# The last spreading of the inverses issued behind their sending, and the last four tiles sent in the order 0, 2, 1, 3: a kernel of attention and a gated linear unit

## The chip, the cores and the metric

The kernel runs on one core of a Trainium2 chip. The metric is the device time of one launch in microseconds; smaller is better. The kernel before takes 1583.95 us, the median of 3 runs (1583.82 to 1584.93). The engines are named as in the profile: PE (TensorE, matmuls; PEld is its loading of weights), DVE (VectorE), ACT (ScalarE), POOL (GpSimd) and SP (SyncE, which here issues all DMAs; a row with SPq is SP's queue).

## The reference

Two branches share the input `x` (2048 rows of 512) and are mixed row by row by a sigmoid gate. The attention has 32 query heads of 16 columns and a single head of keys and values.

```python
g = sigmoid((x * gate_w).sum(-1, keepdims=True))
# a: q in 32 heads of 16; one k, one v
scores = einsum("bhqd,bkd->bhqk", q, k) * 16 ** -0.5
o = einsum("bhqk,bkd->bhqd", softmax(scores), v)
a = o.reshape(1, 2048, 512) @ wo
# b: GLU with a sigmoid gate, 1792 wide
b = (sigmoid(x @ w_gate) * (x @ w_up)) @ w_down
return g * a + (1 - g) * b
```

## The kernel before

**Tiles and units.** The 2048 rows are cut into four blocks of 512 (NB), and the attention of a block into 8 units of four heads (NG), 32 units in all (NU). Operands that need float32 accuracy are held as a high and a low part, and a product is made of three matmuls: high by high, high by low, low by high. The contraction of most matmuls is split over the top and the bottom 64 rows of the array, so two matmuls run beside each other, one in each half. A unit has three phases: score matmuls whose maxima DVE takes (L1141, L1143), score matmuls again whose exponentials ACT takes (L1150, L1152), and groups of 8 value matmuls (L1008, `values`) over 16 chunks of keys.

**What becomes of a unit's result.** The value matmuls give, for each of four heads, 16 columns and the sum of the exponentials. ACT and POOL gather them in `ou` (L1015, L1022). Then, for unit u:

- `store` (L1030, L1031) writes the sums and the results to DRAM (`sd`, `od`);
- `sums` (L1036) reads the sums back in a shape that uses all partitions, `invert` (L1045) takes their inverses on DVE;
- `send_inverse` (L1049) writes the inverses to DRAM (`rd`);
- `spread` (L1055) reads each inverse back, repeated over the 16 rows of its head, into `bc`. For unit NU-2 alone it does so for both halves of the partitions, and also reads the results `od` into `vd` (L1057), so it issues four DMAs there, each of 128 KB;
- `divide` multiplies the two on POOL (L1063) and splits the product into the high and the low part of `o` (L755, L756).

Units are divided in pairs. Of the last pair, unit NU-2 goes through `divide` alone; unit NU-1 stays in its PSUM bank and is handled by the tail. `o` of unit NU-2 is multiplied by the last rows of `wo` (held as `we` in two parts) in jobs of kind "e": L1115 in `fill`, 12 matmuls, added by DVE (L1072).

**What sets the order.** All instructions are emitted in an order worked out ahead. `State` is a planner: it goes through the written string ORDER, one code a step, and each code names what PE does next (a value group, or a matmul for each half of the array). The planner keeps a clock for each engine and for SP and the DMAs. Work that follows from something (a store, an inverse, a spread) is an event with a due time, and is emitted at the first step whose time is past it; POOL's work is a list of tasks, run when the planner's POOL is free. Each engine then runs its own instructions strictly in the order in which they were emitted; SP too, so a DMA issue that waits holds up every issue behind it.

**The half-turn markers.** A job accumulates into two banks, and the two halves of the array change banks in the middle. Where one half has ended its first bank, `fill` places an empty instruction on SP (`nc.sync.nop()`, L1119) that waits for PE's matmul, and the other half's first matmul into that bank waits for it.

**The events that the change touches.** `send` and `issue` advance the planner's SP and DMA clocks and return the time at which a transfer counts as landed (SP's end + SMALL at least); SAFE is 300 more. `send_inverse` makes `spread` due at that time; `spread` makes the task `divide` due 2 * SAFE after its own. Between the emission of `send_inverse` and that of `spread` for unit NU-2, one marker of L1119 is emitted.

**The tail.** After the last step, unit NU-1 is transposed, divided and transposed back (L1178 to L1191), multiplied by its 64 rows of `wo` (L1196), and added to the four last output tiles: tile 1 by ACT and POOL (L1202, L1203), tiles 0, 2 and 3, in this order, by DVE (L1205). SP then sends the four tiles (L1207), in the order 0, 1, 2, 3, each [128, 512] in float32 (256 KB).

Of the kernel before, what the change touches and what calls it, by code (L numbers as in the profile page):

```python
# [12 lines left out]
ALU = mybir.AluOpType  # L13
# [4 lines left out]
S, D, H, DH, F = 2048, 512, 32, 16, 1792  # L18
P = 128
# [7 lines left out]
NU = NB * NG  # L27
# [30 lines left out]
ISSUE, SMALL, TEN_KB, LAST, SAFE, SURE = 185, 750, 20, 300, 300, 150  # L58
# [64 lines left out]
class State:  # L123
# [170 lines left out]
    def event(self, what, args):  # L294
        self.acts.append((what, *args))
        if what == "load_x":
            self.x_loaded[args[0]] = self.send(KC, 1024)
        elif what == "store_q":
            at = self.send(2, 512)
            self.q_ready[tuple(args)] = at  # L300
            self.ba_release(("query", *args), at)
        elif what == "send_max":
            self.after(self.issue(SEND_SQUARE, 16) + SAFE, "place_max", *args)
        elif what == "max_square":
            self.after(self.on("dve", self.now, SQUARE) + TAIL, "send_max", *args)
        elif what == "place_max":
            self.max_ready[args[0]] = self.issue(PLACE, 16) + 150
        elif what == "store":
            at = self.sums_free[args[0] % OU] = self.issue(470, 264) + SAFE
            self.after(at, "sums", *args)  # L310
        elif what == "sums":
            self.after(self.issue(430, 136) + 2 * SAFE, "invert", *args)
        elif what == "invert":
            self.after(self.on("dve", self.now, INVERSE), "send_inverse", *args)
        elif what == "send_inverse":
            self.after(self.send(1, 8) + SAFE, "spread", *args)
        elif what == "spread":
            u = args[0]
            at = self.issue(250, 128)
            if u % 2 or u == NU - 2:  # L320
                self.task(2, at + 2 * SAFE, "divide", u)
        elif what == "out":
            self.tile_free[self.tile_of[tuple(args)]] = self.send(1, 256)
# [401 lines left out]
def tile_kernel(ctx, tc, x_in, wq, wkv, wo, wg, wu, wd, consts_in, out):  # L725
    nc = tc.nc
# [445 lines left out]
    n0 = (NB - 1) * NT  # L1172
    spare = lambda name: ap.tile([P, TB], F32, tag="p", name=name, bufs=PB)
    end, rest = banks[end], [bank for i, bank in enumerate(banks) if i != end]
    ps = rest[3:]
# [16 lines left out]
    for i in range(2):  # L1192
        for j in range(4):
            for t in (2 * i, 2 * i + 1):
                r, m = HALF[t % 2], slice(32 * j, 32 * j + 32)
                nc.tensor.matmul(ps[t][m, :], o[i][r, m], WS["last"][r], start=True, stop=True)  # L1196
    BL = [BA.pop((NB - 1, t)) for t in range(NT)]
    for t in (1, 0, 2, 3):
        ba, g = BL[t], gsig[:, n0 + t:n0 + t + 1]
        if t == 1:  # L1200
            pa = spare("pa_last")
            nc.scalar.activation(pa, ps[t], AF.Copy, scale=g)  # L1202
            nc.gpsimd.tensor_tensor(ba, ba, pa, op=ALU.add)  # L1203
        else:
            nc.vector.scalar_tensor_tensor(ba, ps[t], g, ba, op0=ALU.mult, op1=ALU.add)  # L1205
    for t in (0, 1, 2, 3):
        nc.sync.dma_start(out[(n0 + t) * P:(n0 + t + 1) * P, :], BL[t])  # L1207


    last = {}  # L1210
# [46 lines left out]
```

## Time and profile before

| | us |
|---|---|
| median of 3 runs | 1583.95 |
| lowest and highest run | 1583.82, 1584.93 |
| the profiled execution | 1582.52 |
| its span (first to last instruction) | 1580.7 |
| mean granted clock of PE, of 1 | 0.998 |

| engine | busy us | share of the span |
|---|---|---|
| PE | 1567.2 | 99% |
| DVE | 1338.9 | 85% |
| ACT | 1232.2 | 78% |
| POOL | 803.8 | 51% |

All times in rows of the trace are in us from the start of the span. A row of a timeline has: start, duration, engine, line, operation, what is written <- what is read, shape, count, and in brackets the idle time of the engine before it with what ended it. A row of waits has: who waits <- for whom, total, how often, longest. A table by stretches has: the stretch, its length, busy time of PE, PEld, DVE, ACT and POOL with the number of instructions, then the granted clock of PE, the share of the 16 DMA engines that is busy, and GB/s. A DMA issue's duration is that of the issue; the transfer comes after it. A busy PE is not PE at its peak, and some matmul records can be missing.

### The profile page before, as it was taken

To read this page: it belongs to the slowest core of one execution; us is meant where nothing else is said; L and a number is where in the kernel's file an instruction comes from. 1 tells how busy PE (TensorE), PEld (TensorE's weight loads), DVE (VectorE), ACT (ScalarE), POOL (GpSimd) and SP (SyncE) were. 2 spreads that over 40 slices of the span, in tenths; PEclk is the share of its full clock that TensorE was granted. 3 is DMA by queue.
4 is the path that set the end of the run, shared out by engine and by line. 5 is a ranking of instruction groups with operands and counts; after the bars stand their busy time and mean duration, and the time that the engine had idled before them with its cause. 6 is when DMAs were issued, how large, how long until landed. Compare 5 with 4: busy or idle time off the path is not lost.

```text
span 1580.7 us, 33642 instructions
## 1 busy us (share of the span) xinstructions
PE 1567.2 (99%) x12910; PEld 1009.0 (64%) x12910; DVE 1338.9 (85%) x2277; ACT 1232.2 (78%) x2429; POOL 803.8 (51%) x727
## 2 busy tenths in 40 slices
PE   9999999999999999999999999999999999999997
PEld 7766666666666666666666666667675666656653
DVE  6899899988898888889798888888889888988841
ACT  4277878788788787878788777878878887878895
POOL 4353472655574164367475346275547517357351
PEclk9999999999999999999999999999999999999999
DMA  7421120222122121122122212021213202111011
GB/s 245 169 88 51 35 86 16 66 62 83 43 83 66 36 79 53 35 76 71 45 83 63 64 49 78 18 67 60 77 46 92 65 23 87 46 40 59 18 53 40
DMA packets 63076, 103.43 MB, mean 65 GB/s; under 512 B 24530, under 2 KB 24786, under 8 KB 62916
## 3 DMA queue, kind: packets, MB, share of 16 engines
q1 hardware_dynamic: 62916, 101.29, 20.5%
q8 instruction: 101, 1.65, 0.4%
q14 instruction: 59, 0.48, 0.1%
HBM read 79.51 MB, written 21.75 MB: 64 GB/s over the span
## 4 chain that ended last, share of the span: by engine, by line
PE 96%; DVE 1%; DMA 1%; SPq 1%; ACT 0%; issue 0%; POOL 0%; DVEq 0%; ACTq 0%; POOLq 0%
PE bank L1115 32%; PE bank L1008 29%; PE bank L1141 17%; PE bank L1150 16%; PE bank L853 2%; DVE mx L1143 1%; DMA vd<-od 0%; DMA wqr<-wq 0%; SPq L968 0%; DVE q L948 0%; DMA qs<-qd 0%; ACT x L780 0%; PE bank L1196 0%; DVE x L786 0%; SPq L765 0%
## 5 line engine op out<-in xcount | busy, mean ns | idle before, releaser
L1143 DVE TENSOR_REDUCE mx<-bank 128x1 f32<-128x512 f32 x2048 | 1253.7, 680 | 168.7 <-PE bank L1141 104.0
L1152 ACT ACTIVATE p<-bank 128x512 f32<-128x512 f32 x2048 | 1040.2, 664 | 10.9 <-PE bank L1150 7.7
L1150 PE MATMUL bank<-qs,ks 64*128 64x512 f32 x2048 | 723.7, 399 | 0.0
L1141 PE MATMUL bank<-ks,qs 64*128 64x512 f32 x2048 | 684.2, 404 | 0.5 <-DMA qs<-qd 0.5
L1008 PE MATMUL bank<-p,v_aug 128*32 128x512 f32 x4096 | 480.6, 597 | 0.0
L1141 PEld LDWEIGHTS bank<-ks,qs 64*128 64x128 f32 x2048 | 339.8, 184 | 138.7 <-issue 56.5
L1150 PEld LDWEIGHTS bank<-qs,ks 64*128 64x128 f32 x2048 | 359.6, 184 | 91.3 <-ACT p L1152 27.8
L1015 ACT COPY ou<-bank 128x512 f32<-128x512 f32 x205 | 125.0, 610 | 272.3 <-PE bank L1008 124.1
L1022 POOL TENSOR_TENSOR ou<-ou,ou 128x512 f32<-128x512 f32 x174 | 224.3, 1289 | 170.2 <-ACT ou L1015 167.7
L1115 PE MATMUL bank<-wd,hl 64*128 64x512 f32 x1344 | 272.7, 391 | 0.0
L1115 PE MATMUL bank<-x,wu 64*128 64x512 f32 x1344 | 271.3, 390 | 0.6 <-SPq L1119 0.4
L1008 PEld LDWEIGHTS bank<-p,v_aug 128*32 128x32 f32 x4096 | 113.1, 109 | 248.4 <-issue 220.5
L1115 PE MATMUL bank<-x,wg 64*128 64x512 f32 x1344 | 271.2, 391 | 0.0
L1115 PEld LDWEIGHTS bank<-wd,hl 64*128 64x128 f32 x1344 | 199.8, 184 | 20.6 <-issue 2.5
L1115 PEld LDWEIGHTS bank<-x,wg 64*128 64x128 f32 x1344 | 200.8, 184 | 17.5 <-issue 1.2
L1115 PEld LDWEIGHTS bank<-x,wu 64*128 64x128 f32 x1344 | 201.1, 184 | 17.0 <-issue 2.5
L1094 POOL TENSOR_TENSOR ba<-ba,pa_d 128x512 f32<-128x512 f32 x35 | 44.5, 1283 | 93.2 <-ACT pa_d L1091 93.1
L829 POOL CAST wg<-rg 128x1024 fp32r<-128x1024 f32 x27 | 28.0, 1039 | 123.8 <-PE bank L1115 63.9
L829 POOL CAST wu<-ru 128x1024 fp32r<-128x1024 f32 x27 | 28.1, 1040 | 95.8 <-PE bank L1115 93.2
L756 POOL TENSOR_TENSOR wd<-rd,wd 128x512 fp32r<-128x512 f32 x56 | 72.3, 1292 | 4.5
L756 POOL TENSOR_TENSOR hl<-h,hl 128x512 fp32r<-128x512 f32 x56 | 72.0, 1286 | 4.5
L1115 PE MATMUL bank<-wa,o 64*128 64x512 f32 x360 | 70.4, 391 | 0.0
(80 smaller groups left out, 747.2 us busy)
## 6 DMA issues: line engine op xcount, KB each, us to landing
rg<-wg SPq DMA_DIRECT2D x28, 512.0 KB
ru<-wu SPq DMA_DIRECT2D x28, 512.0 KB
rd<-wd SPq DMA_DIRECT2D x28, 512.0 KB
qs<-qd SPq DMA_DIRECT2D x192, 64.0 KB
qd<-q SPq DMA_DIRECT2D x32, 256.0 KB
od<-ou SPq DMA_DIRECT2D x31, 256.0 KB
xf<-x_in SPq DMA_DIRECT2D x16, 256.0 KB
vd<-od SPq DMA_DIRECT2D x32, 128.0 KB
```

The lines of the kernel that those rows point to most:

```text
L756: lo.tensor_tensor(hl[:, 1, :], raw, f32(hl[:, 0, :]), op=ALU.subtract)
L829: nc.gpsimd.tensor_copy(WS[item][:, 0, :], raw)
L853: nc.tensor.matmul(ps, w[:, p, part(kc)], X[b, kc][:, q, :], start=i == 0, stop=i == 3 * KC - 1)
L1008: nc.tensor.matmul(ps[32 * j:32 * j + 32, :], v_aug[:, c, :], PT.pop((u, c, j)), start=start, stop=stop)
L1015: nc.scalar.copy(to, ps)
L1022: nc.gpsimd.tensor_tensor(SUMS[u], SUMS[u], PARTS_OF[u].pop(0), op=ALU.add)
L1094: nc.gpsimd.tensor_tensor(BA[b, t], BA[b, t], PA[b, t].pop(0), op=ALU.add)
L1115: ins = nc.tensor.matmul(banks[i], l, r, start=start, stop=stop)
L1141: nc.tensor.matmul(banks[i], qs_t[u % 3][r, pr, part(qt)], ks[r, kb * 512:(kb + 1) * 512], start=True, stop=True)
L1143: nc.vector.tensor_reduce(MX[u][:, pr, h, qt, kb:kb + 1], banks[i], axis=AX.X, op=ALU.max)
L1150: nc.tensor.matmul(banks[i], ks[r, part(c)], qs_t[u % 3][r, pr, :], start=True, stop=True)
L1152: nc.scalar.activation(p, banks[i], AF.Exp, scale=0.25)
```

## The change

Two places change. In `State.event`, `spread` of unit NU-2 falls due as soon as the planner's SP is done with the issue of `send_inverse`, not at the time at which the transfer counts as landed plus SAFE; the other units stay as they are. In the kernel the read of `rd` still waits for the write. Since `divide` is due a fixed time after `spread`, it is emitted earlier too. In the tail, tile 0 is added in two halves of 256 columns and sent in two DMAs of 128 KB, and the four tiles are sent in the order 0, 2, 1, 3.

```diff
@@ State.event
         elif what == "send_inverse":
-            self.after(self.send(1, 8) + SAFE, "spread", *args)
+            at = self.send(1, 8) + SAFE
+            self.after(self.sp if args[0] == NU - 2 else at, "spread", *args)
@@ tile_kernel, the tail
         else:
-            nc.vector.scalar_tensor_tensor(ba, ps[t], g, ba, op0=ALU.mult, op1=ALU.add)
-    for t in (0, 1, 2, 3):
-        nc.sync.dma_start(out[(n0 + t) * P:(n0 + t + 1) * P, :], BL[t])
+            for r in (slice(0, D // 2), slice(D // 2, D)) if t == 0 else (slice(0, D),):
+                nc.vector.scalar_tensor_tensor(ba[:, r], ps[t][:, r], g, ba[:, r], op0=ALU.mult, op1=ALU.add)
+    for t in (0, 2, 1, 3):
+        for r in (slice(0, D // 2), slice(D // 2, D)) if t == 0 else (slice(0, D),):
+            nc.sync.dma_start(out[(n0 + t) * P:(n0 + t + 1) * P, r], BL[t][:, r])
```

## The prediction

> **What bounds the kernel now.** I read the page first: its span and its 40 slices.
>
> ```profile
> span 1580.7 us, 33642 instructions
> PE   9999999999999999999999999999999999999997
> ```
>
> PE is full in 39 slices and 7 tenths full in the last (39.5 us long). Both edits lie in that last slice, so what they are worth is to be read there alone. I went there with the chain of waits in order of time (start, duration, what).
>
> ```profile
> 1547.39 0.05 PE bank L1115
> ...
> 1549.36 6.18 DMA vd<-od
> ...
> 1559.04 0.79 PE bank L1115
> ...
> 1563.13 0.89 PE bank L1150 x5
> 1564.02 1.85 PE bank L1008 x16
> ...
> 1567.22 3.62 PE bank L1008 x32
> ```
>
> The reader is to see that the chain leaves PE at 1547.4 and is back on it only at 1559.04: in between it runs over the transfers that `spread` issues and over POOL's `divide`, whose three operations make the last product `o` (its high part by L755, its low part by L756). They stand in POOL's timeline.
>
> ```profile
> 1555.69 1.26 POOL L1063 TENSOR_TENSOR vd<-vd,bc 128x512 f32<-128x512 f32 x1 [19.77 <-DMA vd<-od]
> 1557.02 0.61 POOL L755 CAST o<-vd 128x512 fp32r<-128x512 f32 x1
> 1557.71 1.27 POOL L756 TENSOR_TENSOR o<-vd,o 128x512 fp32r<-128x512 f32 x1
> ```
>
> What PE did around that time (two stretches), and then ACT, is in their timelines.
>
> ```profile
> 1549.51 0.39 PE L1150 MATMUL bank<-qs,ks 64*128 64x512 f32 x1
> 1549.74 0.39 PE L1115 MATMUL bank<-wa,o 64*128 64x512 f32 x1
> ...
> 1553.81 0.49 PE L1150 MATMUL bank<-qs,ks 64*128 64x512 f32 x1
> 1557.68 1.22 PE L1115 MATMUL bank<-we,o 64*128 64x512 f32 x4 [3.38 <-POOL o L755]
> ```
>
> ```profile
> 1549.74 5.50 ACT L1152 ACTIVATE p<-bank 128x512 f32<-128x512 f32 x11 [0.45 <-PE bank L1150]
> 1559.90 2.06 ACT L1152 ACTIVATE p<-bank 128x512 f32<-128x512 f32 x4 [4.67 <-PE bank L1150]
> 1563.59 5.99 ACT L1152 ACTIVATE p<-bank 128x512 f32<-128x512 f32 x12 [1.63 <-PE bank L1150]
> ```
>
> PE does nothing for 3.38 us, does the four matmuls that need only the high part, waits again, and takes the fifth, the first with the low part, at 1559.04. ACT, which takes the exponentials, has two holes of 4.67 and 1.63 us in a row of 27 that otherwise follow each other at 0.50. Last, the granted clock (the column of 0 to 1 after POOL, in a table by stretches).
>
> ```profile
> 1555.80:1556.00 0.20, 0.00 (x0) 0.00 (x0) 0.00 (x0) 0.00 (x0) 0.20 (x1) 0.77 0.00 0
> 1562.60:1562.80 0.20, 0.20 (x4) 0.00 (x0) 0.00 (x0) 0.00 (x0) 0.00 (x0) 0.67 0.00 0
> ```
>
> The two rows are the edges: in the first the clock falls from 1.00 to 0.50, in the second it comes back. So the stall has a second price, half clock from 1555.9 to 1562.7. Steps of two matmuls, one in each half of the array, are 0.23 apart at full clock (1549.51, 1549.74), and a group of 8 matmuls of L1008 takes 0.93 (1.85 for 16). What bounds this stage is how late `o` comes.
>
> **The change, part one: `spread` at once.** It adds and removes no instruction. The event of unit NU-2 falls due as soon as SP's planned issue of `send_inverse` is over, instead of after an allowance for the landing. So the four DMA issues come right behind `send_inverse` on SP. What they are moved past, and what decides when they can start, is on SP:
>
> ```profile
> 1540.24 0.32 SPq L1049 DMA_DIRECT2D rd<-rc  x1
> 1547.60 0.57 SPq L1055 DMA_DIRECT2D bc<-rd  x1
> ```
>
> ```profile
> SPq L1119 <- PE bank L1115: 6.9, 1, 6.9
> ```
>
> ```profile
> 1503.02 0.31 SPq L1049 DMA_DIRECT2D rd<-rc  x1
> 1504.43 0.56 SPq L1055 DMA_DIRECT2D bc<-rd  x1
> ```
>
> ```profile
> 1521.37 0.34 SPq L993 DMA_DIRECT2D md<-sq  x1
> 1523.58 1.38 SPq L1001 DMA_DIRECT2D qs<-md  x2
> ```
>
> These are SP's timeline at the change, its one long wait there (total, times, longest), and two other places of its timeline where a DMA reads what the one before it wrote to DRAM. Today SP sits 6.9 us in the half-turn marker of L1119, until PE gets there at 1547.39; the four issues stand behind it though their input has long been written. After the change they stand in front and wait for `rd` alone. That wait isn't shown for this unit. The nearest rows are those of the unit before, the same DMA and size: 1.41 from issue to issue. The upper end is another round trip through DRAM, `md`, at 2.21; a wait of nothing is excluded, since the data must land. I take 1.41, the row of the same transfer: the first issue goes to 1541.65 (1542.45 at the upper end) instead of 1547.60.
>
> From that issue to POOL's start is 1555.69 - 1547.60 = 8.09, most of it the transfers. No other DMA is issued on SP between 1540.6 and 1547.6, so I keep 8.09: POOL starts at 1549.74. The high part is there 1.95 later (1557.02 + 0.61, and some hundredths until PE sees it), at 1551.69; the low part 3.30 later (1557.71 + 1.27), at 1553.04 (1552.5 and 1553.8 at the upper end). POOL is moved past nothing: it sits idle for 19.77 ahead of `divide`.
>
> When does PE want them? ORDER fixes what PE does step by step, and the planner's clocks of PE, DVE and ACT do not hang on the moved event, so PE's order stays: the first high-part matmul goes beside the score matmul of 1553.81, and the first low-part one two steps of 0.23 on, at 1554.27. The spare is 2.1 us for the high part and 1.2 for the low one (1.3 and 0.4 at the upper end). So I cost the wait at nothing; its cover is PE's own work up to 1553.8, and beyond the spare each us late is a us of stall.
>
> What is queued behind the new wait: the marker of L1119. Four issues of some 0.57 and SP is done at 1543.9, and the marker cannot pass before 1547.4 anyway. Cost nothing.
>
> The gain has three pieces. (a) The low-part step goes from 1559.04 to 1554.27: 4.77. (b) With no stall the clock stays at 1.00. From the low-part step to the next pair of L1008 groups (1564.02) PE needs today 4.98. At full clock it is five steps of 0.23, a group of 8 at 0.93 and six score matmuls at 0.89, in all 2.97, to 1557.24; but the sixth takes a bank that the third of DVE's sums frees. The row of these sums:
>
> ```profile
> 1559.87 1.41 DVE L1072 SCALAR_TENSOR_TENSOR ba<-bank,gsig,ba 128x512 f32<-128x512 f32 x2 [6.16 <-PE bank L1150]
> ```
>
> They begin 0.83 after the low-part step and take 0.71 each, so three end at 1557.2, and I put the next groups at 1557.45, 3.18 after that step. Gain 1.80. (c) From there on PE's 6.82 (1570.84 - 1564.02) stay. That puts PE's end at 1564.27, a gain of 6.57. What is late next is ACT: its 27 exponentials, 13.55 in all, run without a hole from 1549.74 to 1563.29, and the last group of L1008 (0.905) can't start sooner, so its end is about 1564.25. The two meet. The holes close only if each exponential's input comes in time: the score matmuls one step after 1554.27, at 1554.50, take 0.49, so theirs is there about 1555.0 against ACT free at 1555.24. The spare is short, and I take off 0.2 for small holes: 6.4. The bounds are 4.8 (the stall alone) and 6.6.
>
> [...] The trace has the clock falling 1.6 us after the last matmul (which ended at 1554.30) in a gap of 3.38. [...]
>
> **Part two: the last tiles.** One sum of DVE is split into two of 256 columns, one DMA into two, and tile 2 goes ahead of tile 1.
>
> ```profile
> 1572.49 0.29 DVE L1187 TENSOR_TENSOR on<-bank,rc_last 128x128 f32<-128x128 f32 x1
> 1574.35 0.75 DVE L1205 SCALAR_TENSOR_TENSOR ba<-bank,gsig,ba 128x512 f32<-128x512 f32 x1 [1.56 <-PE bank L1196]
> ```
>
> ```profile
> 1575.09 1.26 POOL L1203 TENSOR_TENSOR ba<-ba,pa_last 128x512 f32<-128x512 f32 x1 [16.10 <-ACT pa_last L1202]
> ```
>
> ```profile
> 1575.13 0.34 SPq L1207 DMA_DIRECT2D out<-ba  x1
> ```
>
> ```profile
> 1576.38 1.32 SPq L1207 DMA_DIRECT2D out<-ba  x3
> ```
>
> ```profile
> 1578.00:1578.50 0.50, 0.00 (x0) 0.00 (x0) 0.00 (x0) 0.00 (x0) 0.00 (x0) 1.00 1.05 397
> ```
>
> Tile 0 is sent at 1575.13, tile 1 waits for POOL until 1576.35, and with it the other three, which then keep all DMA engines busy (share 1.05). A half sum of 256 columns lies between the 0.29 of 128 and the 0.75 of 512; on the line between them it is 0.45, so the two cost 0.15 more than the whole. The halves are ready at 1574.80 and 1575.25, tile 2 at 1576.0, tile 3 at 1576.75, POOL's tile 1 still at 1576.35. The last three now begin with tile 2 at about 1576.03 and can follow at 0.44 (1.32 for three). Their data runs back to back, so the end moves with the first of them: 0.35 earlier. The bounds: 0.45 sooner, or 0.2 later if the extra issue and the extra half sum both reach the end.
>
> **The sum.** 6.4 + 0.35 = 6.75. The profiled execution took 1582.52 (span 1580.7 and 1.82 around it): 1575.8 after. The median of the runs shown is 1.43 above it, so the forecast is 1583.95 - 6.75 = 1577.2. If the half clock lasted longer in those runs than in the profiled one, the change takes part of the 1.43 too, and the time falls towards 1575.8.
>
> **The rivals.** First, `o` still comes late. For it: the wait for `rd` and the transfers have one row each. Against: 1.2 us of spare, on a queue with nothing else. At 4 us for `rd` the low part comes at 1555.6, PE stalls 1.35, and the time is 1578.6; if the clock falls in that stall, 1.8 more, 1580.4.
>
> Second, the stall goes and the clock's part doesn't: 4.8 + 0.35 gives 1578.8. For it: the low clock outlasts the stall by 5 us of busy PE (1557.7 to 1562.7). Against: it fell inside the stall. [...]
>
> Third, the change does not move the issues, because a wait that the trace doesn't name holds SP where it is; then only part two counts, 1583.6. Against: the marker has 6.9 us of wait by name.
>
> Fourth, slower: the new wait stands at SP's head and the marker of L1119 behind it, which PE's second half-turn needs from 1549.74 (the step after the last of the first halves). The point from which it decides is the landing of `rd`: up to 7.36 us after its issue (1547.60 - 1540.24) nothing is lost. At 10, the four issues start at 1550.2, the marker passes at 1552.5, PE stalls 2.8 there, and `o` is 2.6 later than today: 1586.5. Against: 1.41 and 2.21 in the rows.
>
> **How the numbers follow.** Forecast 0.76 (its own range 1576.0 to 1578.2), late `o` 0.10, clock without gain 0.05, no move 0.05, slower 0.04. A measurement of this kernel tells about 0.2% from no change, 3.2 us, so faster means under 1580.8. Faster: 0.76 + 0.10 + 0.05, less 0.03 for a late `o` that eats more; same: the no move and that 0.03; slower 0.04. The range goes from 1575.4 (the gain of 6.75, part of the 1.43, and noise) to 1580.2, which takes in the clock rival and most of the late one, and leaves out under 0.2.
>
> **What would show it.** In the changed kernel's timelines: L1055 on SP 1.4 to 2.2 after L1049, ahead of the marker; POOL's L1063 some 8.1 after that; no matmul of L1115 on `we` waiting for POOL; the clock at 1.00 to the tail; ACT's 27 exponentials with holes under 0.3 in all; five issues of L1207. The forecast is wrong if POOL's L756 ends after PE is done with the score matmul beside the first `we` one, if the clock dips without a stall, or if ACT's holes stay.

## The result and the profile after

The changed kernel takes 1575.44 us, the median of 4 runs (1574.79 to 1576.74), against 1584.44 us for the kernel before in the same comparison (4 runs, 1583.82 to 1586.09). The ratio is 0.9947, with a 95% interval of 0.9934 to 0.9960: 9.0 us less, between 6.3 and 10.5. The forecast was 1577.2 in a range of 1575.4 to 1580.2, so the direction was right, the time lies 0.04 us inside the lower end of the range, and the change gave some 2 us more than the 6.75 that were worked out. The profiled execution of the changed kernel took 1574.79, with a span of 1573.0.

On SP the order differs from the one before in two places only: one marker of L1119 now stands behind the four issues of `spread` instead of ahead of them, and the tail has a fifth issue. ACT's instructions stand in the same order as before. The line numbers after are one to three higher than before (L1055 is L1056, L1115 is L1116, L1150 is L1151, L1207 of the sending is L1210).

SP's timeline after, at the place that was moved:

```profile
1538.82 0.32 SPq L1050 DMA_DIRECT2D rd<-rc  x1
1540.27 0.57 SPq L1056 DMA_DIRECT2D bc<-rd  x1
1540.89 0.55 SPq L1058 DMA_DIRECT2D vd<-od  x1
1541.49 0.51 SPq L1056 DMA_DIRECT2D bc<-rd  x1
1542.04 0.51 SPq L1058 DMA_DIRECT2D vd<-od  x1
```

The four issues start 1.45 us behind the sending of the inverses, where 1.41 was taken; before it was 7.36. What comes of them is in POOL's, PE's and ACT's timelines of the same kernel:

```profile
1548.46 1.30 POOL L1064 TENSOR_TENSOR vd<-vd,bc 128x512 f32<-128x512 f32 x1 [13.67 <-DMA vd<-od]
1549.83 0.61 POOL L756 CAST o<-vd 128x512 fp32r<-128x512 f32 x1
1550.52 1.30 POOL L757 TENSOR_TENSOR o<-vd,o 128x512 fp32r<-128x512 f32 x1
```

```profile
1552.73 0.49 PE L1151 MATMUL bank<-qs,ks 64*128 64x512 f32 x1
1552.73 0.96 PE L1116 MATMUL bank<-we,o 64*128 64x512 f32 x5
1553.53 0.39 PE L1151 MATMUL bank<-qs,ks 64*128 64x512 f32 x2
```

```profile
1548.62 13.50 ACT L1153 ACTIVATE p<-bank 128x512 f32<-128x512 f32 x27 [0.46 <-PE bank L1151]
1563.42 0.65 ACT L1179 COPY ou_last<-bank 128x256 f32<-128x256 f32 x2 [1.30 <-PE bank L1009]
```

POOL ends the low part at 1551.82. PE runs straight from the score matmul of 1552.73 into the five products with `we`, with no wait in brackets, and takes the first product with the low part two to three steps later, about 1553.30. So the low part is there some 1.5 us before it is wanted. ACT's 27 exponentials are one piece of 13.50 us without a hole; before they were three pieces with holes of 4.67 and 1.63. The granted clock (the 1.00 behind POOL's count) stayed whole to the end of the stage:

```profile
1548.00:1555.00 7.00, 7.00 (x60) 4.29 (x60) 2.74 (x4) 6.54 (x15) 3.21 (x3) 1.00 0.01 2
1555.00:1559.00 4.00, 4.00 (x36) 1.47 (x30) 0.83 (x2) 3.95 (x9) 0.00 (x0) 1.00 0.00 0
1559.00:1563.00 4.00, 4.00 (x39) 1.23 (x35) 0.75 (x1) 3.12 (x7) 0.00 (x0) 1.00 0.00 0
```

Two distances measure the change without what lies ahead of it. The first, which I call the stage, goes from the start of that score matmul to the start of the first copy of the tail (`ou_last`). It was 1570.86 - 1553.81 = 17.05 and is 1563.42 - 1552.73 = 10.69: a gain of 6.36 in the two first profiles. The second, the tail, goes from there to the end of the span: 9.84 before, 9.58 after. Together that is 6.62 us. The spans differ by 7.7, since the changed kernel reached the score matmul 1.08 earlier (1552.73 against 1553.81), over instructions that are the same in both.

### The profile page after: what moved, and what is told of

Read it like the earlier page. It is cut to its first block, busy times and chain, and to the rows that moved or that the text cites. A ratio compares the mean times of both kernels' runs of the same rounds, so it can differ in the third digit from the quotient of the medians.

```text
span 1573.0 us, 33645 instructions
## 1 busy us (share of the span) xinstructions
PE 1564.3 (99%) x12910; PEld 1008.8 (64%) x12910; DVE 1339.4 (85%) x2278; ACT 1232.0 (78%) x2429; POOL 803.0 (51%) x727
## 4 chain that ended last, share of the span: by engine, by line
PE 98%; DVE 1%; DMA 0%; issue 0%; ACT 0%; POOL 0%; SPq 0%; DVEq 0%; POOLq 0%; ACTq 0%
PE bank L1116 32%; PE bank L1009 30%; PE bank L1142 17%; PE bank L1151 16%; PE bank L854 3%; DVE mx L1144 0%; DMA xf<-x_in 0%; DVE x L787 0%; DVE ba L1207 0%; PE bank L926 0%; PE bank L1197 0%; POOL wg L830 0%; DVE q L949 0%; DVEq L1256 0%; ACT x L781 0%
## 5 line engine op out<-in xcount | busy, mean ns | idle before, releaser
L1151 PE MATMUL bank<-qs,ks 64*128 64x512 f32 x2048 | 722.8, 398 | 0.0
L1151 PEld LDWEIGHTS bank<-qs,ks 64*128 64x128 f32 x2048 | 359.0, 184 | 91.3 <-ACT p L1153 27.7
L1116 PE MATMUL bank<-wd,hl 64*128 64x512 f32 x1344 | 272.6, 391 | 0.0
L1116 PE MATMUL bank<-x,wu 64*128 64x512 f32 x1344 | 271.0, 390 | 0.4 <-SPq L1120 0.4
L1116 PE MATMUL bank<-x,wg 64*128 64x512 f32 x1344 | 271.2, 391 | 0.0
L1116 PEld LDWEIGHTS bank<-wd,hl 64*128 64x128 f32 x1344 | 199.9, 184 | 20.6 <-issue 2.5
L1116 PEld LDWEIGHTS bank<-x,wu 64*128 64x128 f32 x1344 | 201.1, 184 | 16.4 <-issue 2.5
L1116 PEld LDWEIGHTS bank<-x,wg 64*128 64x128 f32 x1344 | 200.4, 184 | 17.4 <-issue 1.2
L1116 PE MATMUL bank<-wa,o 64*128 64x512 f32 x360 | 70.5, 391 | 0.0
```

Source lines behind the costliest of these rows:

```text
L1116: ins = nc.tensor.matmul(banks[i], l, r, start=start, stop=stop)
L1151: nc.tensor.matmul(banks[i], ks[r, part(c)], qs_t[u % 3][r, pr, :], start=True, stop=True)
```

## The experiments

Two questions were open: whether the clock has the share that was given to it, and where the rest of the 9.0 us lies. The theory is that of the prediction: the stall goes, the half clock goes with it, ACT closes its holes, and PE has a spare of some 1.4 us in front of the low part. The rivals are that the low clock has another cause, that there is no spare (or much more), that the tail holds a part, and that the rest is scatter.

### Each part alone, and the kernel before once more

The spread alone:

```diff
-            self.after(self.send(1, 8) + SAFE, "spread", *args)
+            at = self.send(1, 8) + SAFE
+            self.after(self.sp if args[0] == NU - 2 else at, "spread", *args)
```

> Part one of the change alone; the tail as before. The theory (stall 4.8 us, half clock 1.8 us, little holes) expects 6.4 us less than the kernel before, the first of the four spread issues 1.4 to 1.5 us behind the sending of the inverses, no wait of PE for the last product, the clock at 1.00, and a tail (end of the last value group to the end of the span) of 9.9 us as before. The rival that the 9.0 us measured for the whole change lie all in its two parts expects 8.5 us or more here.

Measured: 1576.02 us (5 runs) against 1584.00 (27 runs), ratio 0.9952 (0.9939 to 0.9966), 5.4 to 9.7 us less. The stage is 1563.60 - 1552.88 = 10.72, the tail 9.9. So nearly the whole gain is in this part. The 8.0 of the medians lies between the 6.4 of the theory and the 8.5 of the rival, and the interval holds both.

The tail alone (the halves and the order 0, 2, 1, 3, with the spread as before):

> Part two of the change alone; the spreading as before. The theory expects a tail 0.25 to 0.35 us shorter (9.5 to 9.6 us from the end of the last value group to the end of the span, against 9.86) and the stall of 3.4 us and the half clock of 5 to 7 us as they were; the time 0.3 us less, which is too little to be measured. The rival that the tail holds part of what was gained above the forecast expects 1 us or more less.

Measured: 1583.56 us (11 runs), ratio 0.9997 (0.9988 to 1.0006). Nothing that can be measured, as expected of 0.3 us. The stall was as before (PE's first wait was 3.53 us), but the half clock lasted 3.4 us, under the 5 to 7 expected, and the tail was longer, 10.0 us, not shorter. SP's timeline there shows why:

```profile
1576.39 0.34 SPq L1209 DMA_DIRECT2D out<-ba  x1
1576.78 1.14 SPq L1209 DMA_DIRECT2D out<-ba  x1
1578.02 0.37 SPq L1209 DMA_DIRECT2D out<-ba  x1
```

The issue of the second half took 1.14 us, where it took 0.42 in the changed kernel's profile, and everything behind it on SP came later. That is the extra issue reaching the end, the lower bound of part two in the prediction; it was seen once in six profiles with the two halves.

The kernel before with nothing changed:

> The kernel before, with nothing changed, for the scatter of what is compared. The theory that what was gained above the forecast is scatter of the start (input transfers that land earlier or later) expects a median within 1.5 us of the other runs of the kernel before, with the point at which the inverses are sent 0.5 to 1.5 us earlier or later than 1540.24, and the rest of the span behind it within 0.5 us of the 40.5 us of the first profile. [...]

Measured: 1583.60 us (11 runs), ratio 0.9998 (0.9989 to 1.0007): no difference. But the expectation does not fit its profile: the inverses were sent 0.9 earlier than in the first profile, as it allows, and yet the span behind them was 42.4 us, not 40.5. The clock was at half for 6.8 us as in the first profile. What was longer was the transfer, which no theory had named:

```profile
1546.84 0.57 SPq L1055 DMA_DIRECT2D bc<-rd  x1
```

```profile
1556.33 1.26 POOL L1063 TENSOR_TENSOR vd<-vd,bc 128x512 f32<-128x512 f32 x1 [21.16 <-DMA vd<-od]
```

```profile
1558.31 2.14 PE L1115 MATMUL bank<-we,o 64*128 64x512 f32 x5 [4.77 <-POOL o L755]
```

From the first issue of the spread to POOL's start are 9.49 us, not 8.09, and PE's first wait is 4.77, not 3.38. So the new theory is that the first profile of before was a short one, and that the change takes away a stall which is often longer.

### Is the clock's share the stall's doing?

```diff
+        if j.key == ("e", NB - 1, 0) and h == 1 and at == 0 and start:
+            for n in range(14):
+                nc.tensor.matmul(banks[i], ks[:, part(0)], ks[:, :512], start=True, stop=True)
         ins = nc.tensor.matmul(banks[i], l, r, start=start, stop=stop)
```

This is the kernel before with idle matmuls in the stall; what they write is overwritten by the product behind them.

> The kernel before with 14 full matmuls of 512 columns put into the stall, ahead of the first product of the last units with wo, into the bank which that product then overwrites. The stall stays as long, PE is busy in it. The theory that the stall is what lowers the clock expects the clock at 1.00 throughout, the product with the low part at the same place as before, and the end of the last value group 1.6 to 1.8 us earlier than in the kernel before, so 1.7 us less. The rival that the clock is low there for another reason expects the half clock again and no gain.

Measured: 1581.24 us (11 runs), ratio 0.9985 (0.9976 to 0.9994), 1.0 to 3.8 us less. PE's timeline, and the table by stretches (the granted clock is the 1.00 behind POOL's count):

```profile
1555.14 3.47 PE L1117 MATMUL bank<-ks 128*128 128x512 f32 x14
1558.81 0.73 PE L1118 MATMUL bank<-we,o 64*128 64x512 f32 x4 [0.20 <-POOL o L755]
1560.16 0.49 PE L1118 MATMUL bank<-we,o 64*128 64x512 f32 x1 [0.62 <-POOL o L756]
```

```profile
1555.00:1559.00 4.00, 3.81 (x17) 2.75 (x18) 0.00 (x0) 1.15 (x3) 2.06 (x3) 1.00 0.06 23
1559.00:1563.00 4.00, 3.38 (x25) 1.58 (x25) 2.07 (x3) 2.06 (x4) 1.10 (x1) 1.00 0.00 0
```

The low part still comes 5.44 us after the score matmul, but the clock stays whole, and from the low part's step to the end of the stage are 10.15 us (1570.31 - 1560.16), where the first profile of before had 11.82 (1570.86 - 1559.04) and the changed kernel has 10.12 (1563.42 - 1553.30). So the half clock is the stall's doing and cost 1.67 us against that profile; the prediction had 1.80.

### How much spare is there?

N extra issues on SP, between the sending of the inverses and the spread of the changed kernel, put the spread off without a wait:

```diff
+        if u == NU - 2:
+            junk = dp.tile([6, P, DH], F32, name="junk")
+            for i in range(6):
+                nc.sync.dma_start(junk[i], consts[:, :DH])
         for r in (0, 64) if u == NU - 2 else (64 * (u % 2),):
```

> The changed kernel with 6 more DMA issues (8 KB each, from a constant to DRAM, read by nobody) between the sending of the inverses and the spread, so that the spread starts about 1.1 us later. The theory (a spare of 1.4 us at the low part: ready at 1551.8, wanted at 1553.3 in the changed kernel) expects no wait of PE and no loss against the changed kernel. A rival with no spare (each us of the queue is a us of time) expects 1.1 us more.

> The same with 10 issues, a spread about 2.6 us later. [...] The rival that the spread has still much more spare expects nothing.

> The same with 14 issues, a spread about 4.1 us later. The theory expects PE to wait about 1.8 us for the high part and to take the low part 2.6 us late. [...]

An extra issue took 0.47 us, not the 0.37 on which these expectations rest, so the spread started 3.27, 5.11 and 7.03 us after the sending, against 1.45 without: delays of 1.8, 3.7 and 5.6 us. Measured: 1577.42 (10 runs), 1578.75 (6) and 1583.65 (10), against 1583.69 (23); ratios 0.9966 (0.9956 to 0.9977), 0.9971 (0.9960 to 0.9982) and 0.9998 (0.9989 to 1.0007).

PE's timeline with 6 extra issues and with 10:

```profile
1553.76 0.73 PE L1120 MATMUL bank<-we,o 64*128 64x512 f32 x4
1555.12 0.49 PE L1120 MATMUL bank<-we,o 64*128 64x512 f32 x1 [0.62 <-POOL o L757]
```

```profile
1553.80 0.49 PE L1155 MATMUL bank<-qs,ks 64*128 64x512 f32 x1
1556.23 0.73 PE L1120 MATMUL bank<-we,o 64*128 64x512 f32 x4 [1.94 <-POOL o L756]
1557.59 0.50 PE L1120 MATMUL bank<-we,o 64*128 64x512 f32 x1 [0.62 <-POOL o L757]
```

With 6, PE waits 0.12 us for the high part and 0.62 for the low part, where the expectation had no wait; the low part comes 1.97 after the score matmul instead of 0.57, and the stage is 12.15, 1.45 over the undisturbed 10.7. The clock stayed whole in this profile. The low part is 1.4 late, and that is a sum of four terms: the delay of 1.8, transfers that took 8.48 instead of 8.19, and inverses that were sent only 13.15 us ahead of the score matmul instead of 13.91, less the spare of 1.5 in that profile. So the trace shows a spare that is used up, neither none nor much. The times alone do not refute the rival with no spare: the median is 2.1 over the 1575.32 of the next section's kernel in the same series, about as much as the delay, and the ten runs go from 1575.75 to 1582.93, the last with a mean clock of 0.997.

With 10, the low part is 3.2 late, which the same sum gives (3.7 + 0.4 + 0.7 - 1.5), and the stage is 15.49, 4.8 over. The 1.6 beyond the lateness are the clock, which fell although no single wait of PE was longer than 1.94:

```profile
1558.20:1558.60 0.40, 0.40 (x6) 0.30 (x3) 0.40 (x1) 0.40 (x1) 0.00 (x0) 0.61 0.00 0
1561.40:1561.80 0.40, 0.40 (x2) 0.38 (x4) 0.00 (x0) 0.00 (x0) 0.00 (x0) 0.62 0.00 0
```

The profiled run with 10 is the slowest of its six (1581.67; the others took 1578.00 to 1579.75), and three of the six have a mean clock of 1.000, so the clock does not fall every time.

With 14 the kernel is as slow as before: the spread starts 7.03 us after the sending, where the marker let it start at 7.36. PE's wait and ACT's two holes are back:

```profile
1559.14 2.14 PE L1120 MATMUL bank<-we,o 64*128 64x512 f32 x5 [3.82 <-POOL o L756]
```

```profile
1561.36 2.06 ACT L1157 ACTIVATE p<-bank 128x512 f32<-128x512 f32 x4 [5.15 <-PE bank L1155]
1565.57 5.99 ACT L1157 ACTIVATE p<-bank 128x512 f32<-128x512 f32 x12 [2.15 <-PE bank L1155]
```

The half clock is back too, for 6.8 us (1558.5 to 1565.4). So all of the gain that shows in the time is that of the spread's start, and it is lost again with it.

### The order without the halves

```diff
-            for r in (slice(0, D // 2), slice(D // 2, D)) if t == 0 else (slice(0, D),):
-                nc.vector.scalar_tensor_tensor(ba[:, r], ps[t][:, r], g, ba[:, r], op0=ALU.mult, op1=ALU.add)
+            nc.vector.scalar_tensor_tensor(ba, ps[t], g, ba, op0=ALU.mult, op1=ALU.add)
     for t in (0, 2, 1, 3):
-        for r in (slice(0, D // 2), slice(D // 2, D)) if t == 0 else (slice(0, D),):
-            nc.sync.dma_start(out[(n0 + t) * P:(n0 + t + 1) * P, r], BL[t][:, r])
+        nc.sync.dma_start(out[(n0 + t) * P:(n0 + t + 1) * P, :], BL[t])
```

> The changed kernel with tile 0 added and sent whole; the order 0, 2, 1, 3 stays. The theory that the order gives the gain of the tail and the halves only cost DVE 0.15 us expects the end of the last value group to the end of the span at 9.5 us, 0.1 us under the changed kernel's 9.6. The rival that the halves are what helps expects 9.8 us, as before.

Measured: 1575.32 us (5 runs), ratio 0.9949 (0.9937 to 0.9962); a tail of 1573.5 - 1563.98 = 9.5 us. That fits the order giving the tail's gain and the halves adding nothing, but it is one profile, 0.1 us from tails that scatter from 9.4 to 10.0, so it is not shown. Halves in the old order were not run. The kernel is as good as the changed one and simpler, but not measurably better.

### Where the rest of the 9.0 lies

> The kernel before, another profile. So far the stretch from the score matmul ahead of the stall to the end of the last value group took 17.05, 18.83 and 16.47 us with the spread late, and 10.69 to 10.72 with it early and undisturbed. If the first profile of before was a short one, as the median span of its other runs (1581.8 against its 1580.7) suggests, this stretch is mostly above 17.05, with transfers of the spread that take over 8.1 us or three windows of half clock (a mean clock of 0.997). The rival, that the extra lies ahead of the stall, expects 16.5 to 17.1 again.

> The kernel before, a third profile in this call's series. A stretch above 17.05 us by the theory that the first profile was a short one; 16.5 to 17.1 by the rival that the extra lies ahead of the stall.

> The kernel before, one more profile. A stretch above 17.05 us by the theory that the first profile was a short one; 16.5 to 17.1 by the rival that the extra lies ahead of the stall.

> The changed kernel again. The theory expects the stretch from the same score matmul to the end of the last value group at 10.7 us, whatever the transfers of the spread take within the spare of 1.4 us, a mean clock of 0.999 or 1.000 in nearly every run, and a median 8 us under the kernel before. If the first comparison's 9.0 us was mostly chance, the median is 7 us or less under it.

The three of the kernel before, each with one run, took 1585.10, 1584.30 and 1583.67. The changed kernel took 1576.77 (5 runs) against 1583.31 (9 runs), ratio 0.9957 (0.9943 to 0.9970): 4.8 to 9.0 us less, and 6.5 by the medians. The stages of the three are all above 17.05, as the theory that the first profile was a short one expected. But 6.5 is not the 8 that was expected of the changed kernel; it is under the 7 that was named for a first comparison that was mostly chance. The first of the three, in SP's, POOL's, PE's and ACT's timelines:

```profile
1548.22 0.57 SPq L1055 DMA_DIRECT2D bc<-rd  x1
```

```profile
1557.72 1.26 POOL L1063 TENSOR_TENSOR vd<-vd,bc 128x512 f32<-128x512 f32 x1 [21.19 <-DMA vd<-od]
```

```profile
1554.43 0.50 PE L1150 MATMUL bank<-qs,ks 64*128 64x512 f32 x1
1559.71 2.14 PE L1115 MATMUL bank<-we,o 64*128 64x512 f32 x5 [4.78 <-POOL o L755]
```

```profile
1573.56 0.65 ACT L1178 COPY ou_last<-bank 128x256 f32<-128x256 f32 x2 [1.38 <-PE bank L1008]
```

All profiles with the spread where it was, and the four with it early and undisturbed, read in the same way (us; the low part is that of PE's first product with it):

| kernel | first issue to POOL | score matmul to low part | low part to end of stage | stage |
|---|---|---|---|---|
| before, first profile | 8.09 | 5.23 | 11.82 | 17.05 |
| tail alone | 8.23 | 5.38 | 11.09 | 16.47 |
| before again | 9.49 | 6.62 | 12.21 | 18.83 |
| before, 2 | 9.50 | 6.64 | 12.49 | 19.13 |
| before, 3 | 9.59 | 6.72 | 11.62 | 18.34 |
| before, 4 | 8.16 | 5.30 | 12.44 | 17.74 |
| mean of the six | 8.84 | 5.98 | 11.95 | 17.93 |
| stall kept warm | 8.28 | 5.44 | 10.15 | 15.59 |
| changed | 8.19 | 0.57 | 10.12 | 10.69 |
| changed, again | 8.11 | 0.57 | 10.15 | 10.72 |
| spread alone | 8.25 | 0.57 | 10.15 | 10.72 |
| order alone | 8.59 | 0.57 | 10.14 | 10.71 |

The stage of the kernel before goes from 16.5 to 19.1; that of the early spread does not move by 0.05, though its transfers vary by 0.5. Two things make the scatter of before. The transfers take about 8.2 us in three of the six profiles and 9.5 in the other three, and the second column is the first less 2.85 to 2.87 in each: the marker ties the start of the spread to PE's own progress, so every us of transfer is a us of stall. And the half clock costs between 0.9 and 2.3 us (the third column less 10.15): it lasted 3.4 us in the profile of the tail alone (1559.9 to 1563.3) and about 6.8 in the other five. The shorter one, by its two edges:

```profile
1559.80:1560.00 0.20, 0.06 (x2) 0.06 (x2) 0.00 (x0) 0.00 (x0) 0.12 (x2) 0.80 0.00 0
1563.20:1563.40 0.20, 0.20 (x3) 0.00 (x0) 0.20 (x1) 0.20 (x2) 0.00 (x0) 0.67 0.00 0
```

My guess of three such stretches was an estimate from a mean clock of 0.997 (0.003 of 1583 us are 4.7 us lost, some 9.5 us at half clock), and it was wrong: the three profiles with 0.997 had about 6.8 us as well.

By these means the change saves 17.93 - 10.71 = 7.2 in the stage. The tail is 9.82 in the mean of seven profiles with the old tail (9.74 to 9.90) and 9.6 in the mean of six with the new one (9.4 to 10.0), 0.2 less. That makes 7.4 us, which lies in both intervals, that of the first comparison (6.3 to 10.5) and that of the second (4.8 to 9.0). Ahead of the stage, the score matmul starts at 1554.3 in the mean of the six late profiles and at 1553.2 in the mean of the four early ones, 1.1 earlier, which would make 8.5 us. Single profiles scatter there by up to 2.9, over the same instructions, so I take this 1.1 and what is left of the first comparison's 9.0 for scatter; no run shows that they are.

## Why the prediction was right, and what was mis-sized

**What bounds the kernel.** Right. With the spread moved, PE's stall, the half clock and ACT's two holes all went, and with the spread put off by 5.6 us all came back.

**The new wait and its landing.** 1.45 us measured for 1.41 taken. Nothing was lost behind it on SP: with the early spread the four issues are over at 1542.55, and PE shows no wait for a marker in the stage. The spare in front of the low part was forecast at 1.2 us; it is 1.5 in the first profile of the changed kernel, 1.2 in the second, 0.9 with the order alone and 0.6 with the spread alone. It hangs on how early the inverses are sent (13.05 to 13.91 us ahead of the score matmul) and on the transfers. Transfers of 9.5 us were not seen with the spread early; by these numbers they would cost some 0.7 us where the spare is 0.6, an estimate.

**(a) The low-part step.** Forecast 4.77. By the two first profiles it is 5.23 - 0.57 = 4.66, because the first step behind a value group takes 0.33 and not 0.23. By the mean of the six profiles it is 5.41. This is the mis-sized term: it rests on 8.09 us from the issue to POOL, one row of one profile, and half of the profiles have 9.5 there. The prediction asked what the new wait costs if the transfers are slow after the change, and never what the old stall costs where they were slow before it.

**(b) The clock.** Forecast 1.80; 1.67 with the stall kept warm against the first profile, 1.80 against the mean of the six. The rival without the clock's part is refuted by the run with the idle matmuls (clock 1.00, and 10.15 us from the low part to the end of the stage, where the first profile had 11.82). The run with 10 extra issues lowered the clock with waits of 1.94 and 0.62 in the stage. The half clock, where there was one in the stage, lasted 3.4 us in two profiles (the tail alone and 10 extra issues) and 6.8 in the other six; how long a wait it takes is not shown.

**(c) ACT.** Right that ACT's work and PE's meet, and that the holes close. The 0.2 taken off for small holes did not occur: in the first profiles the stage gained 6.36, for 6.4 forecast, because (a) and (b) came out 0.1 smaller each and (c) 0.2 larger.

**Part two.** 0.35 forecast, about 0.2 measured, within the bounds given; that the order alone does it fits one profile. One profile showed the lower bound's mechanism, the extra issue.

**The sum and the range.** 6.75 forecast for the change, 6.62 in the two first profiles, 7.4 by the means, 9.0 (6.3 to 10.5) and 6.5 (4.8 to 9.0) by the two comparisons. The text did say that the median's 1.43 over the profiled execution might in part be the stall's, but left it out of the forecast and used it for the range alone; so the lower end of the range holds the first comparison's time by 0.04 us, which is luck; the second comparison's 1576.77 lies well inside. The mechanism does not hang on that: each of its steps shows in the traces.

**The slower rival.** Not seen. A landing that decides it was not produced: the delays here put the spread off, not the marker behind a wait of SP for data.

## What to carry to other kernels

Where a stall is to be removed, its size in one profile is a sample: take several profiles of the kernel before, since here the stage with the stall, which hangs on transfers (8.1 to 9.6 us) and brings half clock (3.4 or 6.8 us), scattered from 16.5 to 19.1 us, and without it stayed at 10.69 to 10.72. In an in-order queue, ask for each late issue what stood in front of it; here a marker that waited for PE held four DMA issues whose input had landed, by the runs without the marker in front, some 6 us earlier. And a PE stall of a few us (first waits of 1.9 to 4.9) had a second price here, the half clock, which began in it or up to 0.7 us behind it, cost 0.9 to 2.3 us, and can be measured by itself by filling the stall with idle matmuls.

## What was not expected of the hardware

- The same four transfers of 128 KB, with nothing else issued beside them, took 8.1 to 8.2 us or 9.5 to 9.6 from the first issue to the reader's start, and nothing between, in the kernel before; with the spread early they took 8.1 to 8.6, and up to 8.9 behind extra issues. In the three slow ones the end is drawn out: in the kernel before again the share of the 16 DMA engines falls from 0.22 at 1553.9 to about 0.06, the share of one engine, and 20 to 31 GB/s run on until 1555.7; in the first profile of before it is 0.22 up to 1554.8 and over by 1555.0. Why it is so in half of the profiles was not found.
- With 10 extra issues the clock fell to 0.50, at 1558.3, in a stage in which PE never waited over 1.94 us at a time. The half clock lasted 3.4 us there and with the tail alone, and 6.8 in the six other profiles that show it.
- A DMA issue on SP that takes 0.42 us took 1.14 once, and an issue of 8 KB to DRAM took 0.32 alone and 0.47 in a row of them.
- Ahead of the stage, over the same instructions, the score matmul's start scattered from 1552.73 (changed) to 1555.92 (tail alone).
